# Longformer attention followed by a squared-ReLU expert layer: four reciprocal buffers, scores of two head pairs between expert units, a later pick of the global values, and later loads of batch 2's values

## The chip, the cores and the metric

The kernel runs on one core of one Trainium2 chip. The metric is the device time of one execution in microseconds (us).

The engines are called as in the profile: PE (TensorE, matmuls), DVE (VectorE), ACT (ScalarE), POOL (GpSimd), SP (SyncE, which issues transfers).

## The reference

```python
def _attn_ref(q, k, v, global_idx):            # 8 batches, 8 heads, 576 tokens, 64 wide
    scores = scale * np.matmul(q, k.transpose(0, 1, 3, 2))
    mask = np.abs(pos[:, None] - pos[None, :]) <= 32
    mask = mask | is_global[:, None] | is_global[None, :]     # 8 global tokens
    attn = softmax(np.where(mask, scores, -1e9))              # (written out in the reference)
    return np.matmul(attn, v)

def _moe_ref(x, w_in, w_out):                  # 4608 tokens, 512 -> 2048 -> 512
    r = np.maximum(x @ w_in, 0.0)
    return (r * r) @ w_out
```

The attention result of all batches, with the heads side by side, is the `x` of the expert layer.

## The kernel before

Heads are worked on in four pairs. Queries of a batch are split into two halves. For one pair and half the chain is: `scores` (PE), exponential (ACT, `exps`), product with the band mask (DVE, `masked`), `outputs` (PE: the weighted values and, beside them, the row sums), then `finish_outputs`:

```python
        rec = sbt("rec", [P, 2, GTOK], FP32, bufs=2)
        for r, x, rs, xs in parts:
            act.activation(out=rec[r], in_=av[xs][rs, :, 0:GTOK], func=AF.Ln)      # L702
        act.activation(out=rec, in_=rec, func=AF.Exp, scale=-1.0)                  # L703: 1 / sum
        # ... tensor_reduce of the global columns into gs (DVE, L709) ...
        dve.tensor_tensor(out=xT[...], in0=av[x][...], in1=rec[r], op=ALU.mult)    # L732
```

The columns of the global tokens are computed apart and put into `xT`, the expert layer's input, by eight small copies to addresses held in DVE registers. No expert matmul of a half can start before them:

```python
    def scatter(b, part=None, pairs=slice(0, NHP)):
        # ...
        for g in range(NG):
            dve.tensor_copy(out=xT[:, pairs, lo:hi][:, :, ds(gvs[part][g], 1)],   # L751
                            in_=gxs[b][:, pairs, g : g + 1])
```

The registers are loaded by `load_columns` from values clamped by `columns`. The values of the global tokens are picked from `vb` by five matmuls with one-hot columns and copied to the eight first rows of each of the five value tiles:

```python
    def pick_values():
        for x in range(NT):
            nc.tensor.matmul(gp, oh[:, x, :], vb[0][:, x, 0 : 2 * H : 2], ...)    # L449
        dve.tensor_copy(out=gv16, in_=gp)                                          # L453

    def spread_values(b, op, tiles=range(NT)):
        for x in tiles:
            op(out=vb[b][0:NG, x, 0 : 2 * H : 2], in_=gv16)                        # L457
```

`take(n)` puts the next n units of the expert layer on PE. `keep_warm(n)` puts n filler matmuls there. In the profile before, DVE's instructions from the pick to the reductions stand in the order of the program (the pick's copy at 15.33 us, the spread copies at 16.04, the masks at 17.46, the clamps at 18.55, the reductions at 19.66). The two places that the change reorders are shown with the diff below.

The softmax here doesn't subtract the row's maximum and nothing guards it: scores larger than these inputs give would overflow.

## Time and profile before

| | before |
|---|---|
| time, median of 3 runs | 327.5 us |
| span of the profiled execution | 325.7 us |
| PE busy | 316.4 us, 97 per cent |
| DVE busy | 227.9 us, 70 per cent |
| ACT busy | 214.1 us, 66 per cent |
| first expert matmul of batch 0 / of its second half / of the second token chunk | 25.10 / 38.28 / 69.09 us |

The page cuts the span into 40 slices of 8.1 us; each digit is an engine's busy share of one slice in tenths.

```profile
PE   8989899999999999999999999999999999999996
DVE  8686887787878875987598759885888675313421
DMA  8999999979994999499959997999810010011012
```

PE is full from about the seventh slice on. The digits of 8 are in the first 40 us, where PE waits for the attention of batch 0, and the 6 at the end is the tail. An engine that is 97 per cent busy leaves only its few gaps to be won, so the question is what ends them. The prediction shows those gaps by stretch and by wait.

In what follows three moments measure how far the start of the work has moved: **the first unit** (first expert matmul, just after the first scatter), **the second unit** (first expert matmul of batch 0's second half, just after the second scatter) and **the chunk start** (first matmul of token chunk 1). After the chunk start there are some 253 us of nearly unbroken PE work.

### The profile page before, as it was taken

The page shows a single profiled execution, that of the slowest core. Times are in us where ns is not written, and L with a number is a line of the kernel's source. Part 1 is how long each engine was busy: PE and PEld are TensorE (multiplying, and loading weights), DVE is VectorE, ACT ScalarE, POOL GpSimd, SP SyncE. Part 2 cuts the span into 40 slices and gives each one's busy share as a digit, 9 for nine tenths or more (in the row PEclk, how much of TensorE's full clock was granted, in tenths as well). Part 3 has the DMA queues.
Part 4 walks back from the last instruction along what each step waited for, and adds up shares of the span by engine and source line. Part 5 has one row for each costly group of instructions (what it writes and reads, how often), then busy time and mean ns, then how long its engine had stood idle before and what let it go on. Part 6 is the DMA issues. An engine that isn't in the chain of part 4 may idle for free.

```text
span 325.7 us, 6920 instructions
## 1 busy us (share of the span) xinstructions
PE 316.4 (97%) x2434; PEld 164.4 (50%) x2434; DVE 227.9 (70%) x675; ACT 214.1 (66%) x417; POOL 110.0 (34%) x147
## 2 busy tenths in 40 slices
PE   8989899999999999999999999999999999999996
PEld 3646675445555555445544544455445544444444
DVE  8686887787878875987598759885888675313421
ACT  6687985569954995499549954995499636404600
POOL 9734668039800860089108700780000000000000
PEclk9999999999999999999999999999999999999999
DMA  8999999979994999499959997999810010011012
GB/s 185 174 204 191 166 189 147 137 192 118 140 123 156 79 142 161 137 85 136 129 172 79 134 124 161 97 137 112 156 54 0 34 62 36 2 74 55 2 54 75
DMA packets 148228, 37.53 MB, mean 115 GB/s; under 512 B 136170, under 2 KB 143714, under 8 KB 148194
## 3 DMA queue, kind: packets, MB, share of 16 engines
q0 software_dynamic: 105168, 17.93, 81.1%
q1 hardware_dynamic: 42880, 19.04, 31.7%
q8 instruction: 19, 0.31, 0.4%
q10 hardware_dynamic: 146, 0.13, 0.1%
q14 instruction: 15, 0.12, 0.1%
HBM read 37.30 MB, written 17.05 MB: 167 GB/s over the span
## 4 chain that ended last, share of the span: by engine, by line
PE 85%; DVE 7%; DMA 2%; POOL 2%; ACT 2%; issue 1%; DVEq 0%; ACTq 0%; POOLq 0%
PE mm L587 28%; PE mm L524 26%; PE tr L524 9%; PE tr L587 7%; PE sc L679 3%; PE acc L679 3%; PE sc L627 2%; DMA vb<-in_v_dram 2%; PE mm L543 2%; DVE xT L751 2%; PE acc L627 1%; POOL vb L113 1%; DVE et L643 1%; DVE xT L732 1%; ACT et L636 1%
## 5 line engine op out<-in xcount | busy, mean ns | idle before, releaser
L587 PE MATMUL mm<-w_out,gt 128*128 128x512 f16 x448 | 104.4, 379 | 0.0
L524 PE MATMUL mm<-xT,w_in 128*128 128x512 f16 x384 | 90.8, 379 | 0.2 <-DVE xT L751 0.2
L587 PEld LDWEIGHTS <-gt 128*128 128x128 f16 x560 | 52.4, 98 | 58.6
L524 PEld LDWEIGHTS <-w_in 128*128 128x128 f16 x512 | 47.5, 98 | 53.4 <-issue 0.4
L529 ACT ACTIVATE rl<-mm 128x512 f16<-128x512 f32 x96 | 54.4, 600 | 26.1 <-PE mm L524 26.1
L530 DVE TENSOR_TENSOR gt<-rl 128x512 f16<-128x512 f16 x128 | 51.1, 422 | 16.9 <-ACT rl L529 15.6
L636 ACT ACTIVATE et<-sc 128x880 f16<-128x880 f32 (+1 forms) x32 | 29.0, 906 | 45.7 <-PE sc L627 45.6
L643 DVE TENSOR_TENSOR et<-et,mask 128x880 f16<-128x880 f16 (+1 forms) x64 | 39.0, 615 | 23.4 <-ACT et L636 23.1
L113 POOL DMA_DIRECT2D vb<-in_v_dram x40 | 40.8, 1561 | 8.7 <-DMA w_in<-in_moe_w_in_dram 7.2
L524 PE MATMUL tr<-xT,w_in 128*128 128x512 f16 x128 | 33.0, 380 | 0.0
L564 DVE COPY ot<-mm 128x512 f32<-128x512 f32 (+1 forms) x29 | 19.7, 680 | 18.0 <-PE mm L587 16.3
L636 ACT ACTIVATE et<-acc 128x880 f16<-128x880 f32 (+1 forms) x32 | 29.1, 910 | 1.1 <-PE acc L627 1.0
L703 ACT ACTIVATE rec<-rec 128x288 f32<-128x288 f32 x64 | 28.3, 443 | 2.0
L732 DVE TENSOR_TENSOR xT<-sc,rec 64x288 f16<-64x288 f32 (+1 forms) x55 | 25.0, 455 | 6.5 <-ACT rec L703 6.1
L732 DVE TENSOR_TENSOR xT<-acc,rec 64x288 f16<-64x288 f32 (+1 forms) x55 | 25.0, 455 | 4.1 <-ACT rec L703 1.3
L404 POOL DMA_DIRECT2D scr_k<-in_k_dram x30 | 26.6, 1106 | 3.1 <-issue 3.1
L679 PEld LDWEIGHTS <-vb 128*128 128x128 f16 x288 | 21.3, 98 | 11.6 <-issue 0.2
L925 POOL COPY pin<-gsh 1x1 f32<-1x1 f32 x5 | 0.9, 177 | 75.6 <-DVE gsh L720 75.6
L702 ACT ACTIVATE rec<-sc 64x288 f32<-64x288 f32 (+1 forms) x55 | 22.4, 407 | 5.8 <-PE sc L679 4.2
L404 POOL DMA_DIRECT2D scr_q<-in_q_dram x24 | 24.8, 1567 | 3.2 <-DMA w_out<-in_moe_w_out_dram 3.2
L587 PE MATMUL tr<-w_out,gt 128*128 128x512 f16 x112 | 25.3, 379 | 0.0
L702 ACT ACTIVATE rec<-acc 64x288 f32<-64x288 f32 (+1 forms) x55 | 22.2, 404 | 2.7 <-PE mm L670 0.9
(146 smaller groups left out, 307.7 us busy)
## 6 DMA issues: line engine op xcount, KB each, us to landing
out_dram<-ot SPq DMA_DIRECT2D x35, 256.0 KB
vb<-in_v_dram POOLq DMA_DIRECT2D x32, 120.0 KB, 11.8
scr_q<-in_q_dram POOLq DMA_DIRECT2D x24, 144.0 KB, 5.9
scr_k<-in_k_dram POOLq DMA_DIRECT2D x24, 120.0 KB, 4.2
w_in<-in_moe_w_in_dram POOLq DMA_DIRECT2D x4, 512.0 KB, 11.8
w_out<-in_moe_w_out_dram POOLq DMA_DIRECT2D x4, 512.0 KB, 11.9
natk<-in_k_dram POOLq DMA_DIRECT2D x3, 288.0 KB, 11.0
natq<-in_q_dram POOLq DMA_DIRECT2D x3, 288.0 KB, 11.5
```

The source lines that it names most:

```text
L113: pool.dma_start(out=vb[b][NG : NG + KN[x], x, 2 * hs.start : 2 * hs.stop : 2], in_=v[b, hs, x * KT : x * KT + KN[x]].rearrange("h s d -> ...
L404: pool.dma_start(out=scr[(nm, b % 2)][x * pitch + off : x * pitch + off + hi - lo].rearrange("s (h d) -> s h d", d=D), in_=src[nm][b, :, l ...
L524: nc.tensor.matmul(ph, w_in[:, t, u * P : (u + 1) * P], xT[:, t, XOFF + c * TC : XOFF + (c + 1) * TC], start=(t == 0), stop=(t == NDM - 1),)
L529: nc.scalar.activation(out=rl, in_=ph, func=AF.Relu)
L530: nc.vector.tensor_tensor(out=gts[c][:, u, :], in0=rl, in1=rl, op=ALU.mult)
L587: nc.tensor.matmul(po, gts[c][:, f, m * P : (m + 1) * P], w_out[:, f, :], start=(f == 0), stop=(f == NFF - 1),)
L636: act.activation(out=et[:, :, 0:W], in_=sc[:, :, 0:W], func=AF.Exp, bias=0.0, scale=scale)
L643: dve.tensor_tensor(out=et[:, :, 0:W], in0=et[:, :, 0:W], in1=mask[:, MB[half] : MB[half] + W].unsqueeze(1).to_broadcast((P, 2, W)), op=AL ...
L679: nc.tensor.matmul(banks[e][:, o : o + w], vtf[:, t, vo : vo + P], et[:, e, so : so + w], start=(n == 0), stop=(n == nw - 1), skip_group_c ...
L702: act.activation(out=rec[r], in_=av[xs][rs, :, 0:GTOK], func=AF.Ln)
L703: act.activation(out=rec, in_=rec, func=AF.Exp, scale=-1.0)
L732: dve.tensor_tensor(out=xT[r, hp, x0 : x0 + HS].rearrange("p (k x) -> p k x", k=2), in0=av[x][r, :, 0:GTOK], in1=rec[r], op=ALU.mult,)
```

## The change

The intent is to start the expert stream earlier: the register load leaves the path to the first scatter, four buffers let the logarithms run ahead, the second half's scores are spread between expert units so that their follow-up work on DVE and ACT doesn't bunch up, and the 16-bit key and query transposes of batch 2 get the DMA engines before its values do.

```diff
-SCHED = dict(... h0=0, h1=3, h2=1, h3=0 ...)
+SCHED = dict(... h0=0, h1=1, h4=1, h5=1, h2=1, h3=0 ...)
-        rec = sbt("rec", [P, 2, GTOK], FP32, bufs=2)
+        rec = sbt("rec", [P, 2, GTOK], FP32, bufs=4)
     tr_k(3, then=lambda: tr_q(3, act.copy))
+    half0(2)
     keep_warm(SCHED["w6"])
+    half0(3)
+    columns()
+    load_columns(0)
     pick_values()
-    spread_values(0, dve.tensor_copy)
-    half0(2)
-    half0(3)
+    spread_values(0, dve.tensor_copy, range(0, 4))
+    spread_values(0, act.copy, range(4, NT))
     masked(0, ets[2], WIN)
     masked(0, ets[3], WIN)
-    columns()
-    load_columns(0)
 ... (cut)
     globals_in_place("k")
+    globals_in_place("q")
 ... (cut)
     take(SCHED["h1"])
-    globals_in_place("q")
     half1(2)
     masked(1, ets[2], WIN2)
+    take(SCHED["h4"])
     half1(3)
     masked(1, ets[3], WIN2)
+    take(SCHED["h5"])
+    half1_out(2)
     tr_k(NHP, tag="tr", then=lambda: tr_q(NHP, tag="mm", op=act.copy))
     take(SCHED["h2"])
-    half1_out(2)
+    half1_out(3)
     take(SCHED["h3"])
-    half1_out(3)
     scatter(0, 1)
 ... (cut: inside the loop over batch 1's pairs, after pair hp)
             vb[2] = vb[0]
-            values(2)
             clear_ones(pool.memset, vb[0])
             globals_to_scratch(2)
             transposes(2)
         elif hp == 1:
             value_globals(2)
+        elif hp == 2:
+            pool.tensor_copy(out=pin[0:1], in_=gsum[1][0:1, 0, 2, 0, 0:1])
+            values(2)
```

The last `tensor_copy` is there only to make POOL wait for a reduction of pair 2 before it issues the loads.

More of the change, by code (lines that the diff above doesn't have):

```diff
@@ L42 @@
 MB = (0, 456)
-SCHED = dict(w8=2, w9=3, w5=3, w6=0, w7=4, wa=4, wb=3, wc=3, g0=1, w0=2, w1=4, w2=2, w3=2, w4=3, w=5, h0=0, h1=3, h2=1, h3=0, keep=1, b1=((3, 1, 3), (2, 1, 3), (2, 1, 3), (2, 1, 2)), last=((2, 1, 4), (3, 1, 4), (2, 1, 4), (2, 1, 7)))
+SCHED = dict(w8=2, w9=3, w5=3, w6=0, w7=4, wa=4, wb=3, wc=3, g0=1, w0=2, w1=4, w2=2, w3=2, w4=3, w=5, h0=0, h1=1, h4=1, h5=1, h2=1, h3=0, keep=1, b1=((3, 1, 3), (2, 1, 3), (2, 1, 3), (2, 1, 2)), last=((2, 1, 4), (3, 1, 4), (2, 1, 4), (2, 1, 7)))
 ONES = 2.0**-7 * (1.0 + 15360.0 / 2**23)
```

## The prediction

> **What bounds the kernel now.** The page gives PE 316.4 us of a 325.7 us span, so I first asked where PE is not full, with the table of engine busy time by stretch, cut at the moments where a new kind of work starts on PE.
>
> ```profile
> core 0: us, PE busy (x) PEld busy (x) DVE busy (x) ACT busy (x) POOL busy (x), PEclk, DMA share, GB/s
> 0.00:25.10 25.10, 20.93 (x324) 11.42 (x325) 19.89 (x88) 17.25 (x35) 16.89 (x34) 1.00 1.31 188
> 25.10:38.28 13.18, 12.02 (x163) 8.99 (x163) 9.60 (x26) 11.47 (x23) 6.47 (x9) 1.00 2.06 170
> 38.28:69.09 30.81, 30.15 (x344) 17.95 (x345) 24.39 (x79) 20.40 (x43) 16.94 (x23) 1.00 1.68 166
> 69.09:325.66 256.57, 253.31 (x1604) 126.02 (x1603) 174.02 (x485) 165.00 (x319) 69.69 (x81) 1.00 1.01 99
> ```
>
> Columns: stretch, length, busy time of each engine. From 69.09 us on PE lacks 3.26 us, nearly all of it the tail after the last matmul (the chain of waits ends with a copy at 322.44 us). So 257 us are PE alone and the change touches nothing there. What can be won is in the first 69 us, and it is won only if PE's later stream starts earlier. PE's own waits say where:
>
> ```profile
> PE mm L543 <- DVE xT L751: 2.0, 2, 1.0
> ...
> PE mm L670 <- DVE gs L709: 1.0, 1, 1.0
> PE sc L627 <- DVE xT L751: 0.4, 1, 0.4
> ```
>
> (waiter, releaser, us in total, times, longest). The two waits of L543, at 25.10 and 38.28 us, are the expert layer waiting for the scatter of global columns into xT, first for the first half of batch 0, then for the second. Before each, PE also runs filler matmuls or the rest of its units, so PE time there is not the bound: the chain through DVE and ACT is. Its first part, from the chain of waits in order of time:
>
> ```profile
> 14.91 0.39 PE mm L449
> ...
> 15.33 0.69 DVE gv L453
> ...
> 16.04 1.49 DVE vb L457 x5
> 17.53 1.09 DVE et L643 x2
> ...
> 18.78 0.79 DVEq L741
> ...
> 19.66 0.26 DVE gs L709 x2
> ```
>
> The values pick, five spread copies, two mask products, then 0.79 us in which DVE's queue loads registers (plus 0.2 of clamps), then the reductions. From 19.66 to the scatter's end at 25.06 DVE is almost without a gap. The second part:
>
> ```profile
> 31.84 0.91 ACT et L636
> ...
> 32.77 0.63 DVE et L643
> ...
> 33.44 0.59 PE acc L670 x12
> ...
> 34.55 0.40 ACT rec L702
> ...
> 35.45 0.47 DVE xT L732
> ```
>
> Both exponentials of pairs 2 and 3 run together at 31.04 to 32.74, so mask, outputs, logarithm, exponential and product of both pairs bunch up behind them; scatter follows from 35.94 to 38.22.
>
> [...] each reduction starts after the logarithm of the same bank (20.79 end, 20.82 start). [...] Here the logarithm of the third pair starts at 20.38, after the product that frees rec ended (0.85 us idle); the fourth bank had nothing to do with it. [...]
>
> **The change part by part.**
>
> *Registers loaded earlier.* Clamps and load (18.55 to 19.6, about 1.05 us with the wait after them) move to DVE's idle time before the pick (1.15 us idle at 15.33). Off the path: -1.05.
>
> *Pick after both scores.* Scores of pair 2 can still start at 13.58; those of pair 3 need qt 3, which ACT finishes at 14.41. So the pick starts about 14.8 and its five matmuls take 0.215 each plus 0.17 to drain: done at 16.0 instead of 15.29. +0.74.
>
> *Spread.* Four copies on DVE, one on ACT (0.60, beside): 1.19 instead of 1.49. -0.30. So the masks end at about 19.04 instead of 18.62, and the reductions start at 19.05 instead of 19.66: -0.6.
>
> *Four rec buffers.* ACT then goes 18.35 logarithm and exponential of pair 0 (0.45 and 0.44 pitch), pair 1 to 20.0, pair 2 to 20.8, no wait for DVE. DVE: reduce 19.05, product 19.25, reduce 19.65, product 20.05 (waits ACT), third reduce 20.45 instead of 20.82. From there to the scatter's end is 4.22 us of DVE work as before: 24.67. Gain by the first expert unit: about 0.4 us. Here ACT eats 0.2 of the 0.6.
>
> *Second half.* Starting PE at 24.72 with the pitches of the trace (expert unit of 8 matmuls 0.92, outputs 0.51, fillers 0.75, scores 0.28): unit, outputs 0, filler, outputs 1 to 27.44; unit to 28.35; scores 2; unit to 29.57; scores 3 to 29.85; unit to 30.8; outputs 2 to 31.3; transposes to 31.95; unit to 32.87; outputs 3 to 33.37 (was 34.04). ACT: exponential of pair 2 from 29.05, of pair 3 from 30.37 to 31.25, the cast of q's globals (0.62) gone from this place to a gap before 24.6. DVE: mask 3 ends 31.85, relu and square of the fourth unit to 32.9, product 2 to 33.4, key copies to 34.2, square to 34.55, product 3 to 35.0, scatter 35.03 to 37.3. Before: 38.22. Gain 0.92 us, of which 0.4 came from the first part. PE is ready at 36.65, so a wait of about 0.7 stays at this place.
>
> *Until 69 us.* PE's stream and DVE's chain move together by 0.92. The next hurdle is batch 2.
>
> ```profile
> 67.40 0.37 PE L627 MATMUL sc<-qb,kb 64*128 64x160 f16 x6 [0.39 <-DVE xT L751]
> ```
>
> The release named is not it: the record of semaphores has the query transpose landing at 67.07 to 67.23. So PE arrives at 67.0 and waits for the DMA. If only the stream before it moved, up to all of the gain would be lost here. That is what issuing the values later is for. Queue shares from 58 to 60 us, then from 64 to 66:
>
> ```profile
> q1 hardware_dynamic: 727, 0.19, 96.6%
> q0 software_dynamic: 680, 0.08, 70.1%
> ```
> ```profile
> q1 hardware_dynamic: 1380, 0.35, 81.8%
> q0 software_dynamic: 38, 0.00, 3.9%
> ```
>
> Packets, MB, share of the 16 engines' time: with the values (q0) beside them the transposes (q1) move 727 packets in 2 us, nearly alone 1380. There are 4992 packets of transposes in all, about 7.2 us alone. With values held back to the reduction of pair 2 (59.0 before, 58.1 after), the transposes have the engines from 55.4 (last query store landed) to about 58.5, and share after: estimated landing 63 to 65, needed 66.5. Values: issued 58.4 to 62.9 (0.9 each on POOL), landed about 66, needed at outputs of batch 2 (69.95 - 0.92 = 69.0). Both fit. The 0.39 freed on PE buys nothing more, for the next unit waits for the scatter of batch 1, whose chain (65.25 to 69.05, all DVE) moves by the same 0.92.
>
> **Sum:** -0.4 - 0.5 + 0 + 0 = -0.92 us; 327.5 - 0.9 = 326.6 us.
>
> **Rivals.** (a) *Values become the bound.* Slack is about 3 us, and the values before took 10.5 us from last issue (54.34) to landing (64.88) while sharing. If they did so again from 62.5, they would land at 73 and PE would stall 4 us: 330.5 us. Against it: by then the transposes are mostly done and the queue is empty ahead of them. I give it 7 per cent, mostly in milder forms that eat the gain. (b) *The late pick eats the first gain.* The pick ends 0.74 later; if pair 3's scores start later than 14.45 (they need qt 3) or ACT's spread copy delays the logarithms, the first part gains nothing and the sum is -0.5: 327.0. For it: ACT is the tight engine there by my count. (c) *Expert units between the scores remove the second wait altogether.* If DVE gets to product 3 by 34.3, PE would not wait and the second part gains 1.2 instead of 0.5: 325.9. Against it: DVE's list between mask 3 and the scatter is full. (d) *PE bound anyway.* After 69 us PE is full, so no faster DVE or ACT helps; all that can be won is the start. That caps the gain at the waits of the first 69 us, near 4 us, so under 2 per cent (6.5 us) whatever happens.
>
> **Range and chances.** Middle 326.6 from the sum; (b) and mild (a) set the upper edge 327.3, (c) the lower 325.8. Two per cent is out of reach by (d); slower by two would need worse than (a). Faster 0.01, same 0.98, slower 0.01.
>
> **What would show it.** In the profile after: the DVE register load before the pick; reductions at about 19.05; first expert unit at about 24.7; third logarithm not waiting for DVE; second scatter end at about 37.3 with a PE wait of some 0.7 us before it; no wait of the batch 2 scores; batch 1's scatter end at about 68.1. Wrong if PE waits for vb near 69 us, if the first unit starts no earlier than 25.0, or if the shift at 38 us is there but gone at 70.

## More of the kernel before

On POOL, in program order between the loads of weights and the next batch, stands `next_in_place`, which matters later:

```python
    def next_in_place():
        for nm in "kqv":
            pool.tensor_copy(out=g16s[nm], in_=grow[nm][:, 1])      # L370, three casts
```

## The result and the profile after

The changed kernel took 326.73 us (median of four runs: 326.57, 326.68, 326.77, 327.83), the kernel before 327.6 us (median of four, 327.36 to 327.95). The ratio is 0.998, with a 95% interval of 0.9956 to 1.0004: the same, within 2 per cent. The ratios here and below are those of the record, from the fast runs of the same rounds; they are near the ratios of the medians and means quoted, but not always equal to them (for c_all the means give 0.9982, the record 0.9976).

The profile fell on the longest of the four runs, 327.83 us, and that has to be seen first. Its busy time by stretch, cut at the same three moments (columns as in the prediction):

```profile
core 0: us, PE busy (x) PEld busy (x) DVE busy (x) ACT busy (x) POOL busy (x), PEclk, DMA share, GB/s
0.00:25.80 25.80, 21.07 (x324) 11.70 (x325) 19.67 (x87) 18.08 (x37) 16.96 (x34) 1.00 1.30 190
25.80:38.59 12.79, 12.15 (x164) 8.72 (x163) 9.58 (x26) 10.66 (x22) 6.43 (x9) 1.00 1.96 174
38.59:69.50 30.91, 30.25 (x345) 17.97 (x346) 23.99 (x79) 21.12 (x43) 17.13 (x24) 1.00 1.64 178
69.50:326.10 256.60, 253.29 (x1604) 126.10 (x1603) 173.80 (x485) 164.51 (x318) 69.69 (x81) 1.00 0.97 97
```

Every moment is later than before: 25.79 for 25.10, 38.59 for 38.28, 69.50 for 69.09. The last stretch is as before to 0.03 us. Taken at its word this profile would say that the change made the start worse. The waits of PE say why it does not (waiter, releaser, us in total, times, longest):

```profile
PE mm L543 <- DVE xT L751: 1.8, 2, 1.2
...
PE mm L213 <- DVE rows L178: 1.1, 1, 1.1
```

The second of them was not among PE's leading waits before. It is at the very beginning, the matmul that spreads the eight global indices over the partitions. In the lists of instructions in order of time (start, length, engine, line, shapes) it stands, first in the profile before, then in the one after:

```profile
2.34 0.16 PE L213 MATMUL mm<-g,ones 1*128 1x8 f16 x1
```
```profile
2.86 0.16 DVE L217 TENSOR_SCALAR g32c<-g 1x8 int32<-1x8 int32 x1 [0.85 <-DMA g<-in_global_idx_dram]
...
3.37 0.16 PE L213 MATMUL mm<-g,ones 1*128 1x8 f16 x1 [1.14 <-DVE rows L178]
```

DVE waited for the 64-byte load of the indices. Its packet began 0.9 us later in this execution (2.53 us for 1.65 us in the records of the DMA engines), and the index matmul ran 1.03 us later. The diff reorders nothing before this point. With those 1.03 us taken off, the first unit is at 24.76 us (24.7 was predicted) and the second scatter ends at 37.5 us (37.3 was predicted). That subtraction is an argument and not a measurement, so the same kernel was run again in the experiments.

The other things that the prediction named are here. The second scatter still ends late, and its first copies are long, as the chain of waits shows (start, length, engine, tile, line):

```profile
35.59 0.47 DVE xT L732
36.08 0.64 DVE xT L751
36.74 0.53 DVE xT L751
37.30 0.19 DVE xT L751
```

The query transpose of batch 2 is issued at 56.11 us (the key transpose at 51.96) and is there at 63.13 us, where it had landed at 67.07 to 67.23 us before. The wait of batch 2's scores is gone from PE's list. The values are all there at 68.4 us, and no wait of PE names them.

### The profile page after: what moved, and what is told of

Same layout as the page of the kernel before. It is cut to its first block, busy times and chain, and to the rows that moved or that the text cites. A ratio compares the mean times of both kernels' runs of the same rounds, so it can differ in the third digit from the quotient of the medians.

```text
span 326.0 us, 6920 instructions
## 1 busy us (share of the span) xinstructions
PE 316.8 (97%) x2434; PEld 164.5 (50%) x2434; DVE 227.0 (70%) x674; ACT 214.4 (66%) x418; POOL 110.2 (34%) x148
## 4 chain that ended last, share of the span: by engine, by line
PE 88%; DVE 7%; ACT 2%; issue 1%; DMA 1%
PE mm L587 29%; PE mm L524 26%; PE tr L524 9%; PE tr L587 7%; PE sc L679 3%; PE acc L679 3%; PE sc L627 3%; PE mm L543 2%; PE acc L627 2%; DVE xT L751 2%; PE tr L197 1%; DVE vb L457 1%; PE sc L670 1%; DVE xT L732 1%; ACT rec L702 1%
## 5 line engine op out<-in xcount | busy, mean ns | idle before, releaser
L564 DVE COPY ot<-mm 128x512 f32<-128x512 f32 (+1 forms) x29 | 19.7, 680 | 18.0 <-PE mm L587 16.3
```

## The experiments

Twelve kernels were run, in four calls; kernels of one call shared a chip and the runs of the kernel before. All gave correct results. "Before" in the tables is the kernel before in the same rounds.

| run | what it is | median, us | before, us | mean difference, us | ratio, 95% |
|---|---|---|---|---|---|
| a_again | the change as it is | 327.12 | 327.92 | -0.84 | 0.9976 (0.9959 to 0.9994) |
| a_rec2 | the change with two rec buffers | 327.43 | 327.92 | -0.36 | 0.9992 (0.9967 to 1.0016) |
| a_values_early | the change with the values as before | 327.50 | 327.92 | -0.47 | 0.9989 (0.9971 to 1.0006) |
| b_rec4 | before with four rec buffers | 327.57 | 327.92 | -0.45 | 0.9989 (0.9971 to 1.0006) |
| b_first | before with four buffers and the new first half | 327.18 | 327.57 | -0.31 | 0.9992 (0.9975 to 1.0010) |
| b_second | before with four buffers and the new second half | 327.33 | 327.57 | -0.22 | 0.9995 (0.9977 to 1.0013) |
| b_values_late | before with the late values | 327.28 | 327.57 | -0.17 | 0.9996 (0.9978 to 1.0015) |
| c_pick_mid | the change with the pick between the two scores | 325.92 | 327.57 | -1.67 | 0.9949 (0.9933 to 0.9966) |
| c_tr_late | the change with the transposes after both outputs | 327.43 | 327.99 | -0.51 | 0.9982 (0.9969 to 0.9995) |
| c_b1 | the change with one expert unit moved later in batch 1 | 326.60 | 327.99 | -1.33 | 0.9960 (0.9948 to 0.9973) |
| c_all | the last three together | 327.07 | 327.99 | -0.59 | 0.9976 (0.9962 to 0.9989) |
| c_pick_b1 | c_pick_mid and c_b1 together | 326.22 | 327.27 | -0.93 | 0.9968 (0.9955 to 0.9982) |

And what their profiles show, in us. "Reductions" is DVE's first reduction of the global columns. The last column is the end of PE's last matmul. Each is one execution, so rows can be compared to about half a microsecond, unless the profile itself names what differs.

| profile | index matmul | reductions | first unit | second unit | second less first | scatter of batch 1 ends | chunk start | PE ends |
|---|---|---|---|---|---|---|---|---|
| before | 2.34 | 19.66 | 25.10 | 38.28 | 13.18 | 69.04 | 69.09 | 322.41 |
| after | 3.37 | 20.22 | 25.79 | 38.59 | 12.80 | 69.44 | 69.50 | 322.80 |
| a_again | 2.33 | 18.71 | 24.31 | 37.39 | 13.08 | 68.02 | 68.08 | 322.01 |
| a_rec2 | 2.33 | 18.77 | 24.09 | 37.35 | 13.26 | 68.79 | 68.84 | 322.37 |
| a_values_early | 2.34 | 18.89 | 24.48 | 37.43 | 12.95 | 68.18 | 68.97 | 322.25 |
| b_rec4 | 2.34 | 19.57 | 24.85 | 37.81 | 12.96 | 68.98 | 69.03 | 322.36 |
| b_first | 2.34 | 18.89 | 24.65 | 37.87 | 13.22 | 68.62 | 68.67 | 321.96 |
| b_second | 2.34 | 19.37 | 24.55 | 37.28 | 12.73 | 68.04 | 68.61 | 321.99 |
| b_values_late | 2.37 | 19.34 | 24.68 | 37.86 | 13.18 | 68.72 | 68.77 | 322.06 |
| c_pick_mid | 2.33 | 18.43 | 23.76 | 36.84 | 13.08 | 67.49 | 67.54 | 320.84 |
| c_tr_late | 2.33 | 18.90 | 24.23 | 37.48 | 13.25 | 69.05 | 69.10 | 322.77 |
| c_b1 | 2.39 | 18.80 | 24.13 | 37.14 | 13.01 | 67.35 | 68.37 | 321.46 |
| c_all | 2.34 | 19.88 | 25.43 | 38.20 | 12.77 | 69.11 | 70.12 | 323.37 |
| c_pick_b1 | 2.34 | 19.92 | 25.45 | 38.13 | 12.68 | 68.34 | 69.39 | 322.30 |

### a_again: the change once more

No edit.

> The changed kernel again, unchanged. My theory: 326.6 to 326.8 us, 0.8 to 0.9 us under before, and the one run of 327.83 us (whose profile has the 64-byte index load landing 0.9 us late) was a late start, not part of the change; if one comes again, its profile or time is about 1 us longer. Rival: the change has no effect and the three short runs were luck; then the median is within 0.2 us of before.

The index matmul is at 2.33 us (2.34 before), and the first unit at 24.31, the second at 37.39, the chunk start at 68.08. So the late start of the first profile was of that execution. The six runs lie at 326.89 to 327.62 us, 0.84 us below the kernel before in the mean, and here the interval (0.9959 to 0.9994) leaves out 1. The chain of waits of the first half:

```profile
14.88 1.19 PE mm L449 x5
...
16.09 0.69 DVE gv L453
...
16.81 0.29 DVE vb L457
...
17.14 0.93 PE mm L670 x20
...
18.09 0.42 ACT rec L702
```

The pick's copy starts at 16.09 us where it was 15.33 (the price of scoring both pairs first), and the first logarithm at 18.09 us where it was 17.86. The reductions start earlier all the same, at 18.71 us for 19.66, because DVE no longer loads registers between the masks and the reductions:

```profile
17.62 1.16 DVE L643 TENSOR_TENSOR et<-et,mask 128x912 f16<-128x912 f16 x2
18.71 0.24 DVE L709 TENSOR_REDUCE gs<-mm 128x8 f32<-128x16 f32 x2
```

The chain now leaves DVE at the first spread copy and goes through PE's outputs and ACT's logarithms.

The second half is different from the prediction. The scatter starts at 34.59 us, which is 10.29 us after the first unit (predicted: 35.03 - 24.72 = 10.31; before: 10.84). But it then takes 2.74 us, not the 2.27 of the prediction. DVE's and POOL's instructions there, first of a_again, then of the kernel before:

```profile
34.59 2.74 DVE L751 COPY xT<-gx 128x4 f16 x8
34.74 0.60 POOL L370 CAST g16sk<-grows 8x512 f16<-8x512 f32 x1
...
35.30 0.60 POOL L370 CAST g16sq<-grows 8x512 f16<-8x512 f32 x1
...
35.85 0.60 POOL L370 CAST g16sv<-grows 8x512 f16<-8x512 f32 x1
```
```profile
35.38 0.60 POOL L370 CAST g16sk<-grows 8x512 f16<-8x512 f32 x1
...
35.94 0.64 POOL L370 CAST g16sq<-grows 8x512 f16<-8x512 f32 x1
35.94 2.28 DVE L751 COPY xT<-gx 128x4 f16 x8
...
36.53 0.60 POOL L370 CAST g16sv<-grows 8x512 f16<-8x512 f32 x1
```

A copy of the scatter takes 0.177 us alone (the median of the sixteen in a_again). In a_again three of the eight took 0.57, 0.53 and 0.52 us, and their ends (35.38, 35.94, 36.49) follow the ends of the three casts by about 0.04 us. In the kernel before two were long, 0.46 and 0.52 us, with ends (36.61, 37.17) about 0.04 us after those of the second and third cast; the first cast was all but over when the scatter began. By what means a cast would hold a copy is not shown, but the two go together: in all fourteen profiles, every copy of the second scatter over 0.3 us ends 0.03 to 0.04 us after a cast (but for one in a_rec2, which ends with a transfer issue on POOL). And the length of the scatter follows the number of casts that it meets: 1.79 and 2.06 us with one, 2.28 to 2.45 with two, 2.61 to 2.74 with three (2.91 in a_rec2, with three and the issue), against 1.65 to 1.66 us for the first scatters in which no copy was held. The old order met one or two casts, the new one, which starts earlier, two or three. No run here moved the casts, so what moving them would gain is open.

### a_rec2: the change with two reciprocal buffers

```diff
-        rec = sbt("rec", [P, 2, GTOK], FP32, bufs=4)
+        rec = sbt("rec", [P, 2, GTOK], FP32, bufs=2)
```

> The change with two reciprocal buffers instead of four. My theory after reading the trace: the third logarithm of the first half starts when ACT is free, 0.19 us after the product that would free a buffer, so two buffers cost 0 to 0.1 us: 326.7. Rival (as I predicted it): four buffers carry the first gain; then 0.3 to 0.4 us are lost: 327.1.

The first unit is at 24.09 us, not later than in a_again (24.31). ACT's third logarithm there, in a_rec2 and then in a_again:

```profile
19.72 0.39 ACT L702 ACTIVATE rec<-acc 128x288 f32<-128x288 f32 x1
```
```profile
19.66 0.39 ACT L702 ACTIVATE rec<-acc 128x288 f32<-128x288 f32 x1
```

Neither line ends in a bracket, so neither waited. With the reductions starting at 18.8 us instead of 19.7, DVE's product of pair 0, which frees the first buffer, starts at 19.07 us and takes 0.46 us: the buffer is back 0.19 us before ACT comes to the third logarithm. So four buffers bring nothing to the first half. In time, a_rec2 is 0.31 us above a_again by the medians, which the intervals don't resolve. In the profiles this is found elsewhere: the scatter of batch 1 ends at 68.79 us against 68.02. ACT started a logarithm at 65.16 us and an exponential at 68.19 us, 0.9 and 1.8 us after the recorded ends of the matmuls that they read. The same is seen in a_again and in others with four buffers (below), so it can't be put on the buffers.

### a_values_early: the change with the values issued as before

```diff
             vb[2] = vb[0]
+            values(2)
 ...
-        elif hp == 2:
-            pool.tensor_copy(out=pin[0:1], in_=gsum[1][0:1, 0, 2, 0, 0:1])
-            values(2)
```

> The change with batch 2's values issued at the old place. My theory: the transposes land near 66.8 to 67.1 us again, PE waits for them some 0.6 us, of which about 0.3 us reach the end (the rest is hidden by the scatter of batch 1 at 68.4): 327.0. Rival A: the scatter hides it all: 326.7. Rival B: the transposes hold the end and the whole gain is lost: 327.5.

PE's wait for the transposes is back and has grown. The profile puts it down to the wrong releaser, as it did before. The semaphore record has lost the landing of the query transpose in this execution, so that it is the transpose is argued: DVE's scatter copy named here was done at 66.74 us, 0.86 us before PE went on, and the last packets of the transposes ended at 66.62 us (66.72 in the kernel before, where the landing is on record 0.4 to 0.5 us later):

```profile
PE sc L627 <- DVE xT L751: 1.4, 1, 1.4
```

It was 0.4 us before: PE now comes to these scores 0.86 us earlier, and the transfers come when they came. From 58 to 60 us they moved 732 packets beside 608 of the values, while in a_again they moved 1020 alone, most of them after 59.2 us. The chunk start comes 0.79 us after the scatter of batch 1, where it comes 0.05 us after it in a_again. The median is 0.38 us above a_again (327.50 and 327.12), near the 0.3 expected and inside the scatter of the runs.

### b_rec4: the kernel before with four buffers only

```diff
-        rec = sbt("rec", [P, 2, GTOK], FP32, bufs=2)
+        rec = sbt("rec", [P, 2, GTOK], FP32, bufs=4)
```

> The kernel before with four reciprocal buffers, nothing else. My theory: DVE goes from product to reduction without a gap there, so an earlier logarithm frees nothing: 327.5, no change. Rival: the buffers are worth 0.3 us or more alone: 327.2.

The ratio, 0.9989 with an interval from 0.9971 to 1.0006, resolves nothing. The first unit at 24.85 us lies among those of the other kernels with the old first half (25.10, 24.55, 24.68). The buffers do free ACT: the third logarithm starts at 19.33 us without a wait, where it was 20.38. But DVE goes from product to reduction without a gap, as expected, and the third reduction comes only 0.19 us earlier, half of that because the first one did.

### b_first, b_second, b_values_late: each part alone

b_first is the kernel before with four buffers and with the first hunk of the main sequence from the diff above (scores, `columns`, `load_columns`, pick, spread on two engines). b_second is the kernel before with four buffers and the second (`globals_in_place("q")` early, units between the scores, outputs before and after the transposes). b_values_late has only the last hunk:

```diff
-            values(2)
 ...
+        elif hp == 2:
+            pool.tensor_copy(out=pin[0:1], in_=gsum[1][0:1, 0, 2, 0, 0:1])
+            values(2)
```

> The kernel before with the reordered first half (pick after both scores, registers loaded earlier, spread on two engines) and four reciprocal buffers; second half and values as before. My theory: first expert unit at 24.7 instead of 25.1 us, and that shift carries on: 0.3 to 0.4 us gained, 327.2. Rival: the late pick gives it back, no gain, 327.5; or the wait of the second half absorbs it.

> The kernel before with pairs 2 and 3 of the second half scored between expert units and the cast of q's globals earlier, and four reciprocal buffers; first half and values as before. My theory: the first unit stays at 25.1, the scatter of the second half ends about 0.45 us earlier, at 37.8; 0.2 to 0.45 us gained in the end (part may go to the wait for the transposes): 327.2. Rival: the transposes take it all, 327.5.

> The kernel before with batch 2's values issued later, nothing else. My theory: the transposes land at about 63 to 64 instead of 67.1 us and PE's wait of 0.39 us at 67.4 goes, but the scatter of batch 1 ends at 69.04 as before, so nothing is gained: 327.5. Rival: the wait was on the path, 0.3 to 0.4 us gained: 327.1.

The mean differences are -0.31, -0.22 and -0.17 us. Each interval holds zero (they are 0.18 per cent, 0.6 us, to either side), so no part is resolved alone; their sum, -0.70, which counts the four buffers twice, is not at odds with the -0.84 of the whole. The profiles say more. In b_first the reductions start at 18.89 us, as in the changed kernel, and the second half keeps its old length, 13.22 us. In b_second the first half is the old one, the second half is 12.73 us long, the shortest with a normal start, and PE then waits 1.2 us at 67.25 us for the transposes: its gain is lost there, as the prediction said for a stream that moves without the late values. In b_values_late the transposes are early, but the next unit waits for the scatter of batch 1, which has not moved.

### c_pick_mid: the pick back between the scores

```diff
     half0(2)
-    half0(3)
     columns()
     load_columns(0)
     pick_values()
     spread_values(0, dve.tensor_copy, range(0, 4))
+    half0(3)
     spread_values(0, act.copy, range(4, NT))
```

> The change, but with the values picked between the scores of pair 2 and those of pair 3. My theory: the late pick costs 0.7 us on DVE's path; with the pick at its old time and the registers still loaded early, the reductions start 0.6 to 0.7 us earlier and so does the first expert unit: 326.1. Rival: ACT (exponential of pair 3, then the spread copy, then the logarithms) becomes the bound and less than 0.3 us is gained: 326.5.

This is the best kernel: 325.92 us (325.66 to 326.17), 1.67 us below the kernel before in the mean, ratio 0.9949. It did not share a chip with a_again, so the difference between these two, about 0.8 us, is only as good as the two comparisons with the kernel before. Its chain of waits in the first half:

```profile
15.00 0.39 PE mm L449
...
15.41 0.69 DVE gv L453
...
17.82 0.42 ACT rec L702
```

The pick's last matmul waits for the values (15.00 us, as in the kernel before), while pair 3's scores run behind it. The pick's copy starts 0.68 us earlier than in a_again, the logarithms 0.27 us earlier. The rest of the 0.68 is lost to POOL: a fill of value rows (16.22 to 16.88 us) lies beside the spread copies, and four of them take 1.22 us to the next instruction, where a_again's started behind that fill and took 0.81. Against that, c_pick_mid's first scatter ended before a transfer issue on POOL got in its way: its last copy took 0.18 us, and a_again's took 0.45 us, to the end of an issue at 24.28 us. Together that is the 0.54 us by which the first unit is earlier (0.28 in the reductions, 0.27 in the scatter). The 0.27 is not the pick's own: a_rec2, c_tr_late and c_b1 have the late pick and a first scatter that no issue held up either. The lead is still 0.55 at the second unit and 0.54 at the chunk start. After that a_again loses another 0.63 us to PE's end (253.94 us from chunk start to end, 253.30 in c_pick_mid), 0.41 of it in one wait behind an exponential that started late, see the next part.

### c_tr_late: the transposes after both outputs

```diff
     half1_out(2)
-    tr_k(NHP, tag="tr", then=lambda: tr_q(NHP, tag="mm", op=act.copy))
-    take(SCHED["h2"])
     half1_out(3)
+    take(SCHED["h2"])
+    tr_k(NHP, tag="tr", then=lambda: tr_q(NHP, tag="mm", op=act.copy))
```

> The change, with the transposes of batch 1's first pair moved behind the outputs of pair 3 and one expert unit. My theory: ACT's query copies (0.72 us) and the unit's relu no longer stand between the two pairs' logarithms, the product of pair 3 comes 0.6 to 1 us earlier, and PE's wait of 0.64 us before the second half's units goes: 0.5 us under the change, 326.2. Rival: DVE's list is as full as before with the key copies in another place, and the scatter ends no earlier: 326.7.

The scatter ended at 37.42 us, no earlier: PE had to wait 0.36 us until 31.42 us for the mask of pair 3, and the scatter ran into all three casts and took 2.62 us. The median, 327.43 us, is no better than the changed kernel's. The rival was right here.

This profile and five others have something that I had not expected. From ACT's list in a_again, and the same exponential in c_pick_mid:

```profile
67.90 0.90 ACT L636 ACTIVATE et<-sc 128x880 f16<-128x880 f32 x1 [2.68 <-PE mm L587]
```
```profile
65.92 0.91 ACT L636 ACTIVATE et<-sc 128x880 f16<-128x880 f32 x1 [1.25 <-PE sc L627]
```

In a_again the scores that it reads end at 66.42 us in the profile, 1.48 us earlier, and the releaser named is a later matmul. The semaphore record shows what ACT waited for: PE's semaphore was counted up only at 67.88 us, and ACT started 0.02 us after that. In c_pick_mid this signal is on record 0.02 us after the scores' end. Such starts, 0.5 to 1.9 us late and each 0.02 to 0.03 us behind a signal of PE, are between 65 and 69.5 us in a_again, a_rec2, b_rec4, c_tr_late (65.42 and 68.41 us), c_b1 and c_all, and not in before, after, a_values_early, b_first, b_second, b_values_late, c_pick_mid and c_pick_b1. So ACT was not slow; the signal came late, or the matmuls ended later than the profile models. In the same six the semaphore record misses many updates in this stretch: it has 190 to 224 between 55 and 71 us, and 282 to 334 in the others, but for a_values_early (210, without a late start). No run varied this, so its cause is open, and so is whether executions that are not profiled have it; it is worth up to some 0.7 us of a run and hides or adds to what the parts do.

### c_b1: one unit fewer behind batch 1's pair 2

```diff
-SCHED = dict(... b1=((3, 1, 3), (2, 1, 3), (2, 1, 3), (2, 1, 2)) ...)
+SCHED = dict(... b1=((3, 1, 3), (2, 1, 3), (2, 1, 2), (2, 1, 2)) ...)
```

> The change, with one expert unit (0.86 us) taken out of the third pair of batch 1 and so left for after the last outputs. My theory: the last chain of batch 1 (logarithm to scatter) starts 0.86 us earlier, and PE has one unit more to do while it runs, so its wait of 0.51 us for the scatter goes: 0.5 us under the change, 326.2. Rival: PE then waits for a bank at batch 2's scores instead, gain under 0.2 us: 326.6.

The scatter of batch 1 ended at 67.35 us and PE had a spare unit to run meanwhile, so its wait for that scatter (0.5 us in the profile after) is gone; a wait of 0.36 us for a mask has come in at 67.92 us, behind a late start of ACT. From the second scatter's end to PE's end it is 284.38 us, 0.3 us less than in a_again (284.67). The time, 326.60 us, is 1.33 us below the kernel before, ratio 0.9960. This one is resolved against the kernel before; whether it is better than the changed kernel is not, as they didn't share a chip.

### c_all and c_pick_b1: the edits together

c_all has the edits of c_pick_mid, c_tr_late and c_b1; c_pick_b1 those of c_pick_mid and c_b1.

> The three together: pick in the middle, late transposes, one unit left over. My theory: the gains add up to 1.5 us under the change: 325.2. Rival: moved forward, PE runs into a transfer (values or transposes of batch 2, landing 67 to 68 us) and half of it is lost: 326.0.

> The change with the pick in the middle and one expert unit left over, without the late transposes (which did not help). My theory: the two gains are at different places (24 us and 68 us) and add up: 0.8 to 1.2 us from the pick and 0.3 to 0.5 us from the unit, so a ratio to before of 0.993 to 0.994, about 325.4 us. Rival: both are paid from the same slack at 68 us (the wait for ACT or the values there), so no better than the middle pick alone: ratio 0.995.

Neither is better than c_pick_mid alone: 327.07 and 326.22 us. Their profiles fell on their longest runs (328.43 and 327.34 us) and show a second thing that varies from one execution to the next. PE's filler matmuls near 7 us, in c_all and then in c_pick_mid:

```profile
7.40 1.03 PE L197 MATMUL tr<-idle 128*128 128x512 f16 x2
```
```profile
7.10 0.61 PE L197 MATMUL tr<-idle 128*128 128x512 f16 x2
```

In c_all two take 1.03 us, start to start 0.43 us; in c_pick_mid two take 0.61 us, and three at 7.97 us take 0.82, which is 0.21 us from start to start. So the fillers of c_all run at half speed here. In c_all and c_pick_b1 PE's last filler at half speed starts at 9.7 to 9.8 us, in the other profiles at 3.7 to 5.2 us (the first profile after: 6.2), and their first units are 1.7 us later than that of c_pick_mid, which has the same first half. So the half speed ended at moments up to some 6 us apart in these profiles; no run varied what sets the moment, so that is open. Three of c_pick_b1's six runs, 325.79 to 325.98 us, lie where c_pick_mid's do, so the two edits together seem to bring nothing beyond the first, which was the rival's expectation. But the lead of c_pick_mid over the changed kernel is not confirmed by them either: c_b1, without the middle pick, was 1.33 us below the kernel before of its rounds, c_pick_b1, with it, 0.93.

## Why the prediction was right or wrong

The time was right: 326.6 us was predicted, 326.73 measured, and the mean gain on the second occasion, 0.84 us, is near the sum of 0.92. How near is partly luck: the interval there runs from 0.2 to 1.3 us, the means of the first occasion differ by 0.66, and the two halves below add up to 0.67. Of the steps in it, some were right, one was credited to the wrong cause, and two sizes were off.

- **Registers loaded earlier, -1.05.** Right. From the end of the masks to the reductions it was 1.04 us before (18.62 to 19.66), and nothing in a_again, where the reductions start at 18.71 us while the second mask drains.
- **Pick after both scores, +0.74.** Right in size, +0.76 us. That rival (b) had something in it shows in c_pick_mid: leaving the pick where it was, while keeping the other edits of the first half, brought the reductions 0.28 us earlier than in a_again, and the best time, though c_pick_b1 did not repeat that. The prediction took the later pick as a price that belonged to the change.
- **Spread, -0.30.** Too small. It took 0.30 us a copy, the mean of the five of before, for the copies' own cost. That mean holds a stay behind POOL's fill (16.13 to 16.79 us): one copy took 0.68 us, the others 0.27 to 0.28, starting about 0.2 us apart. In b_values_late, where the fill ended at 15.90 us, five copies took 1.10 us. In a_again four take 0.81, so the term was -0.68 between these two profiles.
- **"Four rec buffers", 0.4 us at the first unit.** The size was right and the attribution failed. The mean of four profiles with the old first half (before, b_rec4, b_second, b_values_late) is 24.79 us, of six with the new one and a normal start (a_again, a_rec2, a_values_early, b_first, c_tr_late, c_b1) 24.31 us: -0.48. But a_rec2 has it with two buffers. Once the reductions start earlier, the products free the old buffers in time. From reductions to first unit the old ones take 5.31 us in the mean and the new ones 5.49, which is the 0.2 that the prediction let ACT eat.
- **Second half, "scatter 35.03 to 37.3", another 0.5.** This is the mis-sized term. The start was right: 10.29 us after the first unit in all eight profiles with the new order (all but c_tr_late and c_all, whose transposes lie elsewhere), 10.31 predicted, and 10.84 in all four with the old order (before, b_rec4, b_first, b_values_late), so the reordering is worth 0.55 us. The length was taken from before, 2.27 us, as if it were the scatter's own; it was 2.74 in a_again, for one more of POOL's casts fell into it. It is 2.61 us in the mean of the eight and 2.24 in that of the four, which gives 0.37 back. From the first unit to the second the eight take 12.95 us and the four 13.14: a gain of 0.19 us and not 0.5. PE's wait there was 0.93 us in a_again and not 0.7, so rival (c), by which it would have gone, fell too.
- **Until 69 us.** The end of batch 1's scatter was predicted at 68.1 us and was 68.02 in a_again, in part because the first half was better than the prediction in this execution. In other profiles ACT's late starts, which the prediction knew nothing of, moved it to 68.8 and more. So this step is confirmed for the executions without them only.
- **Transposes, 63 to 65.** Right, 63.13 in the profile after. **Values, landed about 66.** Late: 67.3 to 68.4 us in the four profiles whose record of these landings is whole, so the slack before 69 us was about a microsecond or two and not 3. Rival (a) fell, as no wait of PE named the values, but by less than was thought.
- **Rival (d), PE bound anyway.** Right. From the chunk start on, the changed kernel and the one before agree to 0.03 us in PE's busy time, and no experiment came near 2 per cent.

The whole gain is thus made of about 0.5 us from the first half, some 0.2 from the second, and the keeping of both past 67 us by the late values (a_values_early loses 0.38 by the medians). Each of these is at or under the resolution of the timed runs; they rest on the profiles.

## What to carry to other kernels

Before a duration from a profile is put into a forecast, ask what ran beside it: a copy's mean can hold a stay beside another engine's instruction (one of five spread copies took 0.68 us here beside POOL's fill, the others 0.27 to 0.28), and moving the copy changes it (five took 1.49 us before, and 1.10 in b_values_late), so look at POOL's line for the same microseconds. To credit a gain to one of several edits, take that edit out again; the buffers that seemed to be the reason were not. And when an early moment before the first changed instruction differs between two profiles, take a second profile before explaining anything behind it.

## What the traces showed of the hardware

- Copies of 128x4 16-bit elements on DVE took 0.18 us alone; those of the second scatters that took 0.32 to 0.63 us ended 0.03 to 0.04 us after a POOL cast of 8x512 elements (but for the one in a_rec2). A transfer issue on POOL of 0.90 us held a copy only in its last 0.45 us in a_again and in its last 0.6 us in the kernel before (the copies took 0.45 and 0.56 us and ended within 0.03 us of the issue's end); in a_again two copies that started in its earlier part took 0.18 us.
- PE's fillers of 128x512 start 0.43 us apart at first and 0.21 us apart later. The last filler at half speed started at 3.7 to 5.2 us in most profiles, 6.2 in one and 9.7 to 9.8 in two, in which the first expert matmul was 1.7 us later than in c_pick_mid.
- The 64-byte load of indices at the start of the kernel began its packet at 1.65 us in one profile (before) and 2.53 in another (after), and the index matmul that needs it moved by 1.03 us.
- A matmul's signal was on record 0.5 to 1.9 us after the matmul's recorded end between 65 and 69.5 us in six of fourteen profiles, where it held ACT back; in c_pick_mid it was on record 0.02 us after.
